# Other places in SBUF for the K, V and output-projection buffers of a cached attention step

## The chip, the cores and the metric

The kernel runs on one core of a Trainium2 chip. The core has a matrix engine (PE), a vector engine (DVE), a scalar engine (ACT), a general engine (POOL) and a queueing engine (SP), and 16 DMA engines that move data between device memory (HBM) and the on-chip memory SBUF. SBUF has 128 partitions, and a tile occupies the same byte range in each of them. PE writes its results into PSUM, which is organised in banks.

The metric is the device time of one execution in microseconds (us). The kernel before took 670.23 us, the median of three runs from 670.22 to 670.27.

## The reference, cut to what matters

One decoding step of a transformer block is computed for four sequences (B = 4, one token each, width D = 512). A conditioning vector gives six modulation vectors. Attention has 32 heads of width 128 over a cache of 4096 keys and values per head and sequence; a gated MLP follows.

```
mod = (silu(c) @ w_mod)                       # six vectors sa, ca, ga, sb, cb, gb
h   = layernorm(x) * (1 + ca) + sa
q   = (h @ wq) as [B, 32, 1, 128]
p   = softmax(q . k_cache * 128**-0.5)        # k_cache, v_cache: [4, 32, 4096, 128], bf16
o   = p . v_cache
x   = x + ga * (o @ wo)
h   = layernorm(x) * (1 + cb) + sb
x   = x + gb * gmlp(h)                        # w_in [512, 1792], w_out [896, 512]
```

The two caches hold 134 MB each. They are read once, and each element is used once.

## The kernel before, in words

**Tiling.** Work on the caches is cut into 32 items (`NQ`), one for each group of four heads and each sequence. An item has 4 MB of K and 4 MB of V. Each is brought by one DMA: 128 partitions, 32 KB in each, contiguous in device memory. The last item's V comes in five pieces, and its K in two. There are two buffers for K (`kt`) and two for V (`vt`), used in turn; the first V buffer holds `w_mod` at the start and the second holds `wq`.

**Steps of an item.** `scores` multiplies a half of the K buffer in place by the broadcast query `qbc` on DVE, and PE adds up the products over the head's width with 16 matmuls against the identity, reading the K buffer in strides; this is done for both halves. `fold` reduces the result into 128 scores a partition. `softmax` is a chain of short DVE instructions with one exponential on ACT. `values` multiplies the probabilities with the V buffer in 32 matmuls; ACT copies the result out, and `diagonal`, `project` and `apply` carry it through the output projection, whose weights for a group of heads are in `wo_g` (for the last group in `wo_l`). The steps are staggered: in the pass of item i stand the scores of i, the values of i-1 and the projection of i-2.

**What sets the order.** A small recording layer (`Program`) keeps each engine's instructions in the order in which they are written and derives the waits from reads and writes of the same tile. No scheduler moves anything. All large loads are issued on SP's queue in the order K of item i+1, then `wo_g` in some items, then V of item i. A load waits on SP until the buffer that it overwrites has been read by PE. The waits follow from the tile names and the ranges inside a tile, not from where in SBUF a tile lies.

**Where tiles lie.** All tiles come from one pool with one buffer each, made in the order of the `sb.tile` calls; the pool puts them one behind the other in SBUF. A tile's place therefore follows from the sizes of the tiles made before it. In the kernel before, `kt` and `vt` are made first. The places in the built program, in bytes within a partition:

| tile | bytes | place before | modulo 512 |
|---|---|---|---|
| kt0, kt1 | 32768 each | 16512, 49280 | 128 |
| vt0, vt1 | 32768 each | 82048, 114816 | 128 |
| rows (c and x) | 1024 | 147584 | 128 |
| wo_g | 4096 | 161504 | 224 |
| wo_l0, wo_l1 | 2048 each | 165600, 167648 | 224 |
| qbc | 8192 | 170080 | 96 |
| win0, win1 | 10752, 3584 | 179872, 190624 | 160 |
| wout0, wout1 | 4096, 3072 | 194208, 198304 | 160 |

Line numbers in the profile are those of the kernel before. L136 is the helper that records every DVE, ACT and POOL instruction, L141 the one that records a load; L349 is a plain matmul, L355 a weight load by itself and L360 a matmul that follows it.

Of the kernel before, what the change touches and what calls it, by code (L numbers as in the profile page):

```python
# [7 lines left out]
BF16 = mybir.dt.bfloat16  # L8
# [218 lines left out]
def kernel(  # L227
# [17 lines left out]
    P = 128  # L245
    B, _, D = A_x.shape
    _, H, SK, DH = A_k_cache.shape
# [4 lines left out]
    NH = 4  # L252
    G = H // NH
    R = P // NH
    NT = SK // R
# [9 lines left out]
    sb = ctx.enter_context(tc.tile_pool(name="sb", bufs=1))  # L265
    pm = ctx.enter_context(tc.tile_pool(name="pm", bufs=1, space=bass.MemoryType.PSUM))

    def tile2(shape, dtype, name, n=2):
        return [sb.tile(shape, dtype, name=f"{name}{a}") for a in range(n)]

    kt = tile2([P, NT * DH], BF16, "kt")
    vt = tile2([P, NT * DH], BF16, "vt")
    rows = sb.tile([2 * B, D], BF16, name="rows")
    wb_t = sb.tile([1, 2], BF16, name="wb_t")
    ident = sb.tile([P, P], BF16, name="ident")
# [19 lines left out]
    rz_t = tile2([P, NH], F32, "rz")  # L295
    oT = sb.tile([P, NH, B], BF16, name="oT")
    oP = sb.tile([P, NH, B], BF16, name="oP")
    wo_g = sb.tile([P, NH, D], BF16, name="wo_g")
    wo_l = tile2([P, NH // 2, D], BF16, "wo_l")
    modT = sb.tile([P, 6, J, B], F32, name="modT")  # L300
    qbc = sb.tile([P, B, G, DH], BF16, name="qbc")
    x1b = sb.tile([P, 2, J, B], F32, name="x1b")
# [8 lines left out]
    win = [sb.tile([P, j1 - j0, F], BF16, name=f"win{a}") for a, (j0, j1) in enumerate(WJS)]  # L311
    JFS = [(0, 4), (4, JF)]
    wout = [sb.tile([P, j1 - j0, D], BF16, name=f"wout{a}") for a, (j0, j1) in enumerate(JFS)]


    banks = [pm.tile([P, 512], F32, name=f"bank{a}") for a in range(8)]
# [457 lines left out]
```

## Time and profile before

| what | value |
|---|---|
| median of three runs | 670.23 us |
| the profiled execution | 670.11 us |
| its span, first to last instruction | 668.3 us |
| PE busy | 420.4 us (63%) |
| DVE busy | 402.9 us (60%) |
| ACT busy | 41.3 us (6%) |
| main DMA queue | 12640 packets, 282.73 MB, 98.8% of 16 engines' span |
| mean rate | 423 GB/s |
| granted PE clock, mean | 0.772 |

The engines' busy times are sums over their instructions. The DMA share is the time that packets took, as a share of the time of 16 DMA engines. A packet is the part of a load that goes to one partition, and one DMA engine moves it. The chain of work that ended last is followed back from the last instruction, each step to what released it. A load's time to landing runs from its issue on the queue to its end, so the waiting behind other loads is in it.

### The profile page before, as it was taken

To read this page: it belongs to the slowest core of one execution; us is meant where nothing else is said; L and a number is where in the kernel's file an instruction comes from. 1 tells how busy PE (TensorE), PEld (TensorE's weight loads), DVE (VectorE), ACT (ScalarE), POOL (GpSimd) and SP (SyncE) were. 2 spreads that over 40 slices of the span, in tenths; PEclk is the share of its full clock that TensorE was granted. 3 is DMA by queue.
4 is the path that set the end of the run, shared out by engine and by line. 5 is a ranking of instruction groups with operands and counts; after the bars stand their busy time and mean duration, and the time that the engine had idled before them with its cause. 6 is when DMAs were issued, how large, how long until landed. Compare 5 with 4: busy or idle time off the path is not lost.

```text
span 668.3 us, 5909 instructions
## 1 busy us (share of the span) xinstructions
PE 420.4 (63%) x3024; PEld 94.2 (14%) x2065; DVE 402.9 (60%) x475; ACT 41.3 (6%) x115; POOL 3.2 (0%) x17
## 2 busy tenths in 40 slices
PE   2557776665576754576655667656557675557784
PEld 2201110011111101111001111101111110111124
DVE  2177766676456666555756654757655666655662
ACT  1200000000000000000000000000000000000002
POOL 1000000000000000000000000000000000000000
PEclk9988876767888767888766788766788876788885
DMA  9999999999999999999999999999999999999995
GB/s 377 430 426 430 436 430 430 429 437 426 431 431 437 430 426 431 435 430 426 435 435 430 430 431 435 430 428 431 437 428 430 431 437 426 431 431 437 422 410 198
DMA packets 12673, 282.90 MB, mean 423 GB/s; under 512 B 1388, under 2 KB 1908, under 8 KB 3956
## 3 DMA queue, kind: packets, MB, share of 16 engines
q1 hardware_dynamic: 12640, 282.73, 98.8%
q8 instruction: 7, 0.11, 0.1%
q14 instruction: 6, 0.05, 0.0%
q10 hardware_dynamic: 20, 0.01, 0.0%
HBM read 282.73 MB, written 0.00 MB: 423 GB/s over the span
## 4 chain that ended last, share of the span: by engine, by line
DMA 63%; PE 24%; DVE 12%; issue 0%; SPq 0%; ACT 0%; DVEq 0%
DMA kt<-in_A_k_cache_dram 58%; PE bank L360 23%; DVE kt L136 11%; DMA vt<-in_A_v_cache_dram 3%; DMA wout<-in_B_w_out_dram 1%; PE bank L349 0%; SPq L141 0%; DVE S L136 0%; DVE P L136 0%; ACT E L136 0%; DVE mx L136 0%; DVE nm L136 0%; DVE mT L136 0%; DVE hm L136 0%; DVE hb L136 0%
## 5 line engine op out<-in xcount | busy, mean ns | idle before, releaser
L360 PE MATMUL bank<-kt,ident 128*128 128x512 bf16 x1024 | 295.0, 459 | 180.9 <-DVE kt L136 180.9
L136 DVE TENSOR_TENSOR kt<-kt,qbc 128x8192 bf16<-128x8192 bf16 x64 | 282.7, 4420 | 86.6 <-DMA kt<-in_A_k_cache_dram 86.6
L136 DVE TENSOR_REDUCE S<-bank 128x64 f32<-128x512 f32 x64 | 44.3, 692 | 125.6 <-PE bank L360 125.6
L355 PEld LDWEIGHTS <-ident 128*128 128x128 bf16 x64 | 9.1, 142 | 359.4 <-issue 359.3
L349 PE MATMUL bank<-vt,P 128*32 128x512 bf16 x992 | 59.2, 380 | 0.5 <-DMA vt<-in_A_v_cache_dram 0.5
L349 PE MATMUL bank<-sel,osb 128*128 128x4 f32 x248 | 35.7, 267 | 29.4 <-ACT osb L136 25.0
L136 ACT ACTIVATE E<-S,nm 128x128 f32<-128x128 f32 x32 | 12.8, 401 | 568.3 <-DVE nm L136 568.3
L349 PEld LDWEIGHTS bank<-sel,osb 128*128 128x128 f32 x248 | 33.0, 207 | 41.9 <-ACT osb L136 36.9
L136 DVE TENSOR_TENSOR P<-E,mask 128x512 bf16<-128x512 f32 x32 | 22.2, 693 | 18.0 <-ACT E L136 18.0
L349 PEld LDWEIGHTS bank<-rs,ones_f 128*128 128x128 f32 x64 | 12.1, 190 | 104.8 <-issue 104.0
L349 PEld LDWEIGHTS bank<-vt,P 128*32 128x32 bf16 x992 | 23.6, 96 | 21.4 <-DMA vt<-in_A_v_cache_dram 0.6
L136 ACT COPY osb<-bank 128x512 f32<-128x512 f32 x31 | 17.5, 565 | 17.4 <-PE bank L349 17.3
L349 PE MATMUL bank<-vt,hbc 128*32 128x512 bf16 x128 | 8.9, 448 | 4.7 <-DMA vt<-in_A_wq_dram 4.7
L349 PE MATMUL bank<-oP,wo_g 128*128 128x4 bf16 x112 | 3.9, 165 | 10.2 <-DVE oP L136 10.2
L136 DVE RECIPROCAL rz<-bank 128x4 f32<-128x4 f32 x32 | 5.6, 176 | 7.3 <-PE bank L349 7.3
L136 DVE TENSOR_REDUCE mx<-S 128x1 f32<-128x128 f32 x32 | 9.2, 286 | 1.1
L349 PE MATMUL bank<-rs,ones_f 128*128 128x4 f32 x64 | 9.1, 212 | 0.0
L136 DVE STREAM_TRANSPOSE nm<-hb 128x32 f32<-128x32 f32 x32 | 6.8, 212 | 1.1
L136 DVE STREAM_TRANSPOSE mT<-mx 128x32 f32<-128x32 f32 x32 | 6.8, 212 | 1.1
L136 DVE TENSOR_SCALAR rs<-mask,rs 128x4 f32<-128x4 f32 x32 | 7.2, 224 | 0.0
L136 DVE TENSOR_REDUCE hm<-mT 128x1 f32<-128x32 f32 x32 | 6.0, 186 | 1.1
L136 DVE TENSOR_SCALAR hb<-hm 128x32 f32<-128x32 f32 x32 | 5.8, 181 | 1.1
(91 smaller groups left out, 75.5 us busy)
## 6 DMA issues: line engine op xcount, KB each, us to landing
kt<-in_A_k_cache_dram SPq DMA_DIRECT2D x31, 4096.0 KB, 25.8
vt<-in_A_v_cache_dram SPq DMA_DIRECT2D x31, 4096.0 KB, 33.1
vt<-in_A_wq_dram SPq DMA_DIRECT2D x1, 4096.0 KB, 20.5
kt<-in_A_k_cache_dram SPq DMA_DIRECT2D x2, 2048.0 KB, 24.7
wo_g<-in_A_wo_dram SPq DMA_DIRECT2D x7, 512.0 KB, 22.8
vt<-in_w_mod_dram SPq DMA_DIRECT2D x1, 3072.0 KB, 10.2
vt<-in_A_v_cache_dram SPq DMA_DIRECT2D x1, 2048.0 KB, 19.8
win<-in_B_w_in_dram SPq DMA_DIRECT2D x1, 1344.0 KB, 14.8
```

Source lines behind the costliest of these rows:

```text
L136: eng, lambda e: getattr(e, name)(*args, **kw), ins, outs, sem=sem, done=done, after=after,
L349: "PE", lambda e: e.matmul(out, lhsT=lhsT, rhs=rhs, start=start, stop=stop, **kw),
L355: prog.add("PE", lambda e: e.ldweights(lhsT), [lhsT], [], done=False)
L360: return e.add_instruction(mybir.InstMatmult(name=nc.get_next_instruction_name(), engine=mybir.EngineType.PE, ins=[e.lower_ap(rhs), e.lowe ...
```

## The change

Only the order in which tiles are made is changed, and with it their places. The small tiles, `qbc`, `win` and `wout` are made first; then a tile `fill` of 96 bytes that nothing reads or writes; then the two V buffers, the two K buffers, `wo_l` and `wo_g`.

```
-    kt = tile2([P, NT * DH], BF16, "kt")
-    vt = tile2([P, NT * DH], BF16, "vt")
     rows = sb.tile([2 * B, D], BF16, name="rows")
...
-    wo_g = sb.tile([P, NH, D], BF16, name="wo_g")
-    wo_l = tile2([P, NH // 2, D], BF16, "wo_l")
     modT = sb.tile([P, 6, J, B], F32, name="modT")
...
     wout = [sb.tile([P, j1 - j0, D], BF16, name=f"wout{a}") for a, (j0, j1) in enumerate(JFS)]
+    fill = sb.tile([P, 48], BF16, name="fill")
+    vt = tile2([P, NT * DH], BF16, "vt")
+    kt = tile2([P, NT * DH], BF16, "kt")
+    wo_l = tile2([P, NH // 2, D], BF16, "wo_l")
+    wo_g = sb.tile([P, NH, D], BF16, name="wo_g")
```

The places after it, in the built program:

| tile | place after | modulo 512 |
|---|---|---|
| vt0, vt1 | 62208, 94976 | 256 |
| kt0, kt1 | 127744, 160512 | 256 |
| wo_l0, wo_l1 | 193280, 195328 | 256 |
| wo_g | 197376 | 256 |
| rows | 16512 | 128 |
| qbc | 30816 | 96 |
| win0, win1 | 40608, 51360 | 160 |
| wout0, wout1 | 54944, 59040 | 160 |

## The prediction

> **What bounds the kernel now.** I read the chain of work that ended last first, then the DMA part of the page, then the windows of the steady stretch, and last what the DMA queue itself waits for. From the page:
>
> ```profile
> span 668.3 us, 5909 instructions
> ...
> DMA  9999999999999999999999999999999999999995
> ...
> DMA packets 12673, 282.90 MB, mean 423 GB/s; under 512 B 1388, under 2 KB 1908, under 8 KB 3956
> ## 3 DMA queue, kind: packets, MB, share of 16 engines
> q1 hardware_dynamic: 12640, 282.73, 98.8%
> ...
> DMA 63%; PE 24%; DVE 12%; issue 0%; SPq 0%; ACT 0%; DVEq 0%
> ...
> L360 PE MATMUL bank<-kt,ident 128*128 128x512 bf16 x1024 | 295.0, 459 | 180.9 <-DVE kt L136 180.9
> L136 DVE TENSOR_TENSOR kt<-kt,qbc 128x8192 bf16<-128x8192 bf16 x64 | 282.7, 4420 | 86.6 <-DMA kt<-in_A_k_cache_dram 86.6
> ...
> kt<-in_A_k_cache_dram SPq DMA_DIRECT2D x31, 4096.0 KB, 25.8
> vt<-in_A_v_cache_dram SPq DMA_DIRECT2D x31, 4096.0 KB, 33.1
> ```
>
> From the windows of the steady stretch (length, busy time of PE, PE loads, DVE, ACT and POOL, clock, DMA share, GB/s):
>
> ```profile
> 100.00:200.00 100.00, 63.44 (x402) 12.64 (x252) 62.27 (x67) 4.82 (x15) 0.00 (x0) 0.76 1.01 432
> 400.00:500.00 100.00, 61.77 (x402) 12.52 (x252) 60.95 (x67) 4.82 (x15) 0.00 (x0) 0.76 1.00 431
> ```
>
> From the DMA queue's own waits:
>
> ```profile
> SPq L141 <- PE bank L360: 511.5, 31, 27.6
> SPq L141 <- PE bank L349: 91.2, 31, 17.9
> ```
>
> The chain gives PE and DVE a third of the span, but that misleads. It steps from a landed K through multiply and matmuls to the release of the buffer, then into the next load of that buffer, whose 25.8 us are mostly queueing: a 4 MB load alone takes 9.7 us at 432 GB/s. So 16 us of other transfers stand before it, and the 16 DMA engines never stop: share 1.00 in every steady window, 98.8% over the span, while DVE and PE are busy 62 of 100 us. SP waiting for PE costs nothing as long as that queue is full. The kernel's time is the sum of packet times on one DMA engine, from 2 us to 663 us, with about 5 us of arithmetic behind. Any effect must come through the duration of a packet.
>
> **One packet, from the trace's records of single packets.** A 4 MB load is 128 packets of 32 KB, one per partition, eight on each engine. Shortest and mean durations on the main queue, in ns, with the start of the destination modulo 512 bytes (read off the built program):
>
> ```
> size     destination        start   shortest  mean
> 32768    K, V, wq           128     1213      1217.5
> 24576    w_mod              128      912       996
> 16384    K and V, last      128      611       616
>  4096    V, last            128      159       162
>  4096    wo_g               224      159       163
>  4096    wout0              160      159       163
>  2048    V, last            128       84        87
>  1024    wo_l               224       46        50
>  1024    c, x (eight)       128       44        83
>   256    code (other queue)          15        15
> ```
>
> From 16 KB to 32 KB the shortest grows by 602 ns, so the bytes move at 27.2 a ns, and 1213 - 1204 leaves a fixed 9 ns a packet. The rest of the mean, 4.5 ns, is a spread: the first 32 KB load (wq) is 1213 in all 128 packets, later ones mix 1213, 1218 and 1221. On each engine 504 packets have 32 KB; 8 x 1217.5 = 9.74 us, and successive steady loads start 9.71 us apart, so packets overlap by a few ns and a ns off a packet is a ns off its engine.
>
> **The change, part by part.**
> *Order of the work.* No instruction, wait, semaphore or issue is added, removed or moved on any engine or queue: the streams differ in places and in three extra source lines. The fill tile is never read or written. Cost 0, which needs no cover.
> *Small tiles and the other weights* (rows up to qbc and wout). They move down by 131072 bytes as a block and stand as before modulo 512: qbc at 96, win and wout at 160. The temporaries made later shift by 96 bytes; they are touched in microseconds at the two ends. Bounds: an instruction there is some 0.17 us by the rows of DVE, about twenty lie in the last 5 us, and 10% on all would be 0.3 us either way. I take 0.
> *Engines reading K and V.* The multiply in place has kt at 256 instead of 128 and qbc where it was. Its 64 instructions take 4412 to 4427 ns, whichever of two K buffers and two halves; matmuls from V have 379 ns at the median. No place but 128 appears, so the trace doesn't price another. It is hidden by the DMA queue: a pass is 19.4 us long (two loads) and holds 62% of that, 12.1 us, of DVE. The multiply would have to grow from 4.42 to over 8.0 us before DVE sets the pass. Taken at 0, with a loss bounded in the rivals.
> *DMA into K, V and wo.* This is the term. Packets whose start moves to 256 modulo 512, per engine: 504 of 32 KB, 8 of 24, 24 of 16, 8 of 8, 64 of 4 (8 V, 56 wo_g), 16 of 2, 32 of 1 KB: 656. win, two wout and the four little inputs keep their modulus. All shown starts (128, 160, 224) are off a multiple of 256; the trace holds no large packet on one. Upper gain: the whole fixed 9 ns, 656 x 9 = 5.9 us, and beyond it the spread, 504 x 4.5 = 2.3 us. Lower bound: the spread widens, all packets as the slower common value, 1221 instead of 1217.5: 504 x 3.5 = 1.8 us more; the two worst K/V loads average 1222, which on all would be 504 x 4.6 = 2.3 us more. Nearest rows for what the fixed part can shrink to: the 256-byte packets keep 15 - 9.4 = 5.6 ns, and the shortest 1 KB packets of c and x keep 44 - 37.6 = 6.4. The usual is 8.5 (159 - 150.5; 84 - 75.3 = 8.7; 46 - 37.6 = 8.4). I take the lowest, 5.6, so 2.9 ns a packet: 656 x 2.9 = 1.9 us saved. This is the softest step: the packets of c and x start at 128 themselves, so something other than the start can shorten the fixed part.
>
> Sum: the profiled execution took 670.11 us for its span of 668.3 us, 0.12 below the median of 670.23. 670.11 - 1.9 = 668.2; against the median, 668.3 us, 0.28% less.
>
> [...] The 4 KB packets have the same shortest time at 128, 160 and 224. [...]
>
> **The rivals.**
> *Nothing (places don't matter, or less than 1.3 us).* For it: the equal rows at three starts, and a stream already at 432 GB/s, 27.0 a ns an engine against 27.2. Against it: none of these starts is on 256. It gives 670.1 us, 669 to 671.5.
> *Slower: the landing side spreads.* Place: the 32 KB packets into K and V while DVE and PE read neighbouring K and V buffers, whose places all move. For it: packets are uniformly 1213 before the engines work and mixed later; the cause doesn't show. Against it: the second K load, moved from 29 to 39 us with DVE and PE already on the first, still has 115 of 128 at 1213. Price: 1.8 to 2.3 us, 672.0 to 672.5; it decides against no change once the mean of 32 KB packets is over 1220.1 (2.7 ns x 504 = 1.34 us). [...]
> *Much slower: the multiply loses its rate at the new place.* At twice 4.42 us, DVE would have 12.1 + 8.8 = 20.9 us a pass, 1.5 over the DMA's 19.4: about 30 x 1.5 = 45 us more, 715. Against it: its place moves by 128 bytes, by whole multiples of its element, and qbc stays.
> That the moves do not happen is excluded: the built program has K and V at 256 modulo 512.
>
> **How the numbers follow.** Forecast (fixed part shrinks): 0.43, its own range 666.3 to 668.9. Nothing: 0.35. Spread: 0.19, with its tail above 672.5. Multiply: 0.03. The bound for a difference is 0.2%, 1.3 us. So faster 0.43, same 0.35, slower 0.22. For 8 in 10 I go from 666.3 (4.0 us saved: half of the fixed 9 ns and half of the spread, 656 x 4.5 + 504 x 2.2) to 672.4, the upper end of the spread's price; the sides left out hold about 0.05 below and 0.10 above.
>
> **What would show it.** Right: the same instruction counts and chain; 32 KB packets with a shortest near 1210 and a mean near 1214.5; steady windows at 433 GB/s; multiply at 4.42 us and matmul from V at 379 ns; wo_g packets at 156; win and wout unchanged at 140 and 159. Nothing: shortest 1213 and mean 1217.5. Spread: shortest 1213, mean over 1220, windows at 430. Multiply: DVE over 90 of 100 us and DMA share below 1. I would be wrong outright if the steady DMA share fell while no packet lengthened, since then the queue ran dry and the cause is an engine.

## The result, and the profile after

The changed kernel took 666.87 us (median of five runs, 666.79 to 666.96) beside 670.22 us for the kernel before (670.09 to 670.27): a ratio of 0.995 with a 95% interval of 0.9937 to 0.9964. That is 3.35 us less, faster by 0.5%, where 1.9 us less had been forecast. The profiled execution took 666.79 us for a span of 665.0 us.

From the page of the kernel after, the lines that answer to those shown of before (the kernel is three lines longer ahead of them, so L363 is the L360 of before):

```profile
span 665.0 us, 5909 instructions
...
DMA  9999999999999999999999999999999999999995
...
DMA packets 12673, 282.90 MB, mean 425 GB/s; under 512 B 1388, under 2 KB 1908, under 8 KB 3956
## 3 DMA queue, kind: packets, MB, share of 16 engines
q1 hardware_dynamic: 12640, 282.73, 98.8%
...
DMA 62%; PE 24%; DVE 12%; issue 0%; SPq 0%; ACT 0%; DVEq 0%
...
L363 PE MATMUL bank<-kt,ident 128*128 128x512 bf16 x1024 | 293.0, 457 | 179.7 <-DVE kt L136 179.7
L136 DVE TENSOR_TENSOR kt<-kt,qbc 128x8192 bf16<-128x8192 bf16 x64 | 282.7, 4419 | 84.7 <-DMA kt<-in_A_k_cache_dram 84.6
```

From its windows, with the columns as before (length, busy times, clock, DMA share, GB/s):

```profile
50.00:250.00 200.00, 131.00 (x833) 23.90 (x505) 131.07 (x135) 9.64 (x30) 0.00 (x0) 0.77 1.00 433
250.00:450.00 200.00, 123.66 (x830) 24.77 (x530) 124.17 (x135) 9.63 (x30) 0.00 (x0) 0.76 1.00 434
```

The same two windows of the kernel before:

```profile
50.00:250.00 200.00, 132.01 (x827) 25.47 (x505) 130.42 (x135) 9.64 (x30) 0.00 (x0) 0.76 1.01 432
250.00:450.00 200.00, 124.17 (x812) 23.80 (x504) 123.20 (x132) 9.64 (x30) 0.00 (x0) 0.76 1.00 431
```

The structure has not moved: 5909 instructions, the same packets, the same multiply, a DMA share of 1.00. Only the rate is different, by half a percent, and it can just be seen in the last column. The single packets tell more. Shortest, mean (both in ns) and the share of packets above the shortest, for before and after:

```
size     destination   start      shortest      mean               above the shortest
                       before/after             before   after     before  after
32768    K, V, wq      128 / 256  1213 / 1213   1217.5   1213.6    77%     0.3%
 4096    wo_g          224 / 256   159 / 159     162.8    159.6    70%     0.2%
 1024    wo_l          224 / 256    46 / 46       49.7     46.0    63%     0%
 3584    win           160 / 160   140 / 140     146.1    141.3    66%     4%
 4096    wout0         160 / 160   159 / 159     162.6    159.2    69%     3%
```

The shortest packet is what it was in every size. What went is the spread above it, and it went for win and wout0 too, whose starts modulo 512 are unchanged. (The first tile of win comes as three packets of 3584 bytes a partition, the tiles of wo_l as two of 1024.)

The sum of packet times on one engine (all packets of the main queue, divided by 16) fell from 659.99 to 657.20 us, by 2.79 us: 1.96 in the 32 KB packets, 0.63 in the other moved sizes (24 KB 0.14, 16 KB 0.08, 8 KB 0.03, V's last and wo_g's 4 KB 0.20, 2 KB 0.05, 1 KB 0.12, rounded), and 0.20 in win and wout. The 0.14 us of the 24 KB packets (w_mod, the first load) can't be put down to the start: over all fourteen profiles these packets sum to 7.8 to 8.2 us on an engine, in no order of start, and the profile of the change happens to have the lowest sum. The last load packet ended 3.32 us earlier. The other 0.5 us is that the end belongs to the slowest of the 16 engines: before, 16 to 18 load packets are under way at once from 657 to 658.5 us, and from 661 to 662.8 us one (after, one from 658.25 to 659.5 us). The last load packet ended 2.8 us behind that sum before, and 2.3 us behind it after (start and gaps included).

### The profile page after: what moved, and what is told of

Read it like the earlier page. It is cut to its first block, busy times and chain, and to the rows that moved or that the text cites. A ratio compares the mean times of both kernels' runs of the same rounds, so it can differ in the third digit from the quotient of the medians.

```text
span 665.0 us, 5909 instructions
## 1 busy us (share of the span) xinstructions
PE 417.8 (63%) x3024; PEld 93.0 (14%) x2065; DVE 402.7 (61%) x475; ACT 41.2 (6%) x115; POOL 3.2 (0%) x17
## 4 chain that ended last, share of the span: by engine, by line
DMA 62%; PE 24%; DVE 12%; issue 0%; SPq 0%; ACT 0%; DVEq 0%
DMA kt<-in_A_k_cache_dram 58%; PE bank L363 24%; DVE kt L136 11%; DMA vt<-in_A_v_cache_dram 3%; DMA wout<-in_B_w_out_dram 1%; PE bank L352 0%; SPq L141 0%; DVE S L136 0%; DVE P L136 0%; ACT E L136 0%; DVE mx L136 0%; DVE nm L136 0%; DVE mT L136 0%; DVE hm L136 0%; DVE hb L136 0%
## 5 line engine op out<-in xcount | busy, mean ns | idle before, releaser
L363 PE MATMUL bank<-kt,ident 128*128 128x512 bf16 x1024 | 293.0, 457 | 179.7 <-DVE kt L136 179.7
L352 PE MATMUL bank<-sel,osb 128*128 128x4 f32 x248 | 34.2, 261 | 29.4 <-ACT osb L136 24.9
L352 PEld LDWEIGHTS bank<-sel,osb 128*128 128x128 f32 x248 | 31.5, 199 | 41.9 <-ACT osb L136 36.8
```

What stands on the lines that cost most here:

```text
L352: "PE", lambda e: e.matmul(out, lhsT=lhsT, rhs=rhs, start=start, stop=stop, **kw),
L363: return e.add_instruction(mybir.InstMatmult(name=nc.get_next_instruction_name(), engine=mybir.EngineType.PE, ins=[e.lower_ap(rhs), e.lowe ...
```

## The experiments

Three theories for the gain. A: what counts is whether K and V start on a multiple of 256 bytes. B: what counts is the region of SBUF, or the order of the buffers. C: it comes from wo_g and wo_l alone. Beside these stands the question where the spread arises: in the DMA engines, or where DVE and PE use SBUF at the same time.

**The changed order, off 256 again.** K, V and wo all start at 128 modulo 512.

```
-    fill = sb.tile([P, 48], BF16, name="fill")
+    fill = sb.tile([P, 240], BF16, name="fill")
```

> The changed order of tiles, but with a fill of 480 bytes, so that K, V and wo start at 128 modulo 512 again. Theory A (the start of K and V modulo 256 bytes makes the difference): as before, 670.2 us, the mean of 32 KB packets at 1217 ns, shortest 1213. Theory B (it is where in SBUF, or in which order, the buffers lie): as after the change, 666.9 us, packets at 1213.5. Theory C (only wo_g and wo_l matter): wo is off 256 here too, so 670.2 us as with A.

Measured: 670.09 us beside 670.13 before, ratio 0.9999 (0.9989 to 1.0008). 32 KB packets: shortest 1213 ns, mean 1217.46, 76% above the shortest. The whole gain is gone with the new order still in place. B falls.

**The order before, on 256.** K and V at 256, wo_g at 352, win and wout at 288 modulo 512.

```
+    fill = sb.tile([P, 64], BF16, name="fill")
     kt = tile2([P, NT * DH], BF16, "kt")
     vt = tile2([P, NT * DH], BF16, "vt")
```

> The order of before with 128 unused bytes in front, so that K and V start at 256 modulo 512 and everything else moves by 128 bytes (wo_g to 352, win and wout to 288 modulo 512, none on a multiple of 256). Theory A: 666.9 us, packets of 32 KB at 1213.5 ns. Theory B: 670.2 us, 1217. Theory C: 670.2 us, since wo is still off 256.

Measured: 667.14 us beside 670.13, ratio 0.9955 (0.9938 to 0.9971); mean of 32 KB packets 1213.58. 128 unused bytes in front of the K tiles do nearly all of what the change does. C falls: wo is off 256 here. A stands.

**V at 128, K at 256, and the mirror.** In the changed order, first

```
-    fill = sb.tile([P, 48], BF16, name="fill")
+    fill = sb.tile([P, 240], BF16, name="fill")
     vt = tile2([P, NT * DH], BF16, "vt")
+    fill2 = sb.tile([P, 64], BF16, name="fill2")
     kt = tile2([P, NT * DH], BF16, "kt")
```

> The changed order, V at 128 and K and wo at 256 modulo 512. Theory A in its simple form (each packet pays for its own start): half of the effect, 668.5 us, packets into V mixed at 1213 to 1221 with a mean of 1217 and packets into K at 1213. Theory A in another form (misaligned packets spoil the pace of all that follow): packets of both kinds are mixed, between 668.5 and 670.2 us. Theory C: 666.9 us.

Measured: 667.67 us, ratio 0.9962 (0.9948 to 0.9976); mean 1213.83 ns, and only 3% of the 32 KB packets above the shortest. Half of the large packets are misaligned, and hardly any of them is long. Neither form of A as written holds: such a packet does not pay for its own start, nor does it spoil all that follows. The mirror asks whether V is special:

```
     vt = tile2([P, NT * DH], BF16, "vt")
+    fill2 = sb.tile([P, 192], BF16, name="fill2")
     kt = tile2([P, NT * DH], BF16, "kt")
+    fill3 = sb.tile([P, 64], BF16, name="fill3")
     wo_l = tile2([P, NH // 2, D], BF16, "wo_l")
```

> The mirror of the run with V at 128 and K at 256: now V and wo at 256, K at 128. If it is the share and the alternation of such packets that counts, 667.7 us and a mean of 1213.8 ns, as in the mirror. If K's start is the one that matters, 670 us and 1217.

Measured: 667.79 us, ratio 0.9962 (0.9948 to 0.9977), mean 1213.73, 3% above the shortest. Neither tensor is special.

**The same loads without the attention's arithmetic,** at the places of before and then of after. The per-item calls are left out; loads, head and tail stay. The output is not the attention's.

```
-        scores(i, 0)
...
-        scores(i, 1)
...
-        values(i - 1)
...
-    values_last(NQ - 1)
```

> Places of before, but the attention's arithmetic is left out: no scores, softmax, values or projection, so no engine reads or writes K, V or wo between 31 us and the end; the same loads in the same order, each waiting only for the load two earlier into its buffer. If the spread of packets needs the engines' accesses to SBUF, all 32 KB packets are 1213 ns, and successive loads start 9.681 us apart. If it comes from the DMA engines and the start alone, they are mixed at 1213 to 1221 with a mean of 1217, 9.716 us apart.

> The control of the run without the attention's arithmetic (again no scores, softmax, values or projection), with the places after the change. The start alone should set the packets: 32 KB packets at 1213 ns, mean 1213.6, 9.681 us from load to load, and about 665 us where the same with 128 took 668.3. If the arithmetic had a share in the gain, the two would differ by less than 3 us.

Measured, one run each, at 128: 668.33 us, 80% of the 32 KB packets above the shortest, mean 1217.02, loads 9.713 us apart in the median. At 256: 665.32 us, 0.1% above the shortest, mean 1213.13, 9.681 us apart. From the page of the run at 128, busy times and a window of its steady stretch:

```profile
span 666.5 us, 893 instructions
...
PE 18.2 (3%) x325; PEld 11.2 (2%) x325; DVE 8.7 (1%) x52; ACT 10.6 (2%) x20; POOL 3.2 (0%) x17
```

```profile
200.00:300.00 100.00, 0.00 (x0) 0.00 (x0) 0.00 (x0) 0.00 (x0) 0.00 (x0) 0.50 1.00 430
```

The same lines of the run at 256:

```profile
span 663.5 us, 893 instructions
...
PE 17.9 (3%) x325; PEld 11.1 (2%) x325; DVE 8.7 (1%) x52; ACT 10.6 (2%) x20; POOL 3.2 (0%) x17
```

```profile
200.00:300.00 100.00, 0.00 (x0) 0.00 (x0) 0.00 (x0) 0.00 (x0) 0.00 (x0) 0.50 1.01 435
```

In these windows nothing but DMA runs, and at 128 the spread is there as before (80% above the shortest, 77% with the arithmetic). The move by 128 bytes is worth 3.0 us of span here (666.5 against 663.5), and 3.3 us in the whole kernel; with one run each, the 0.3 us between the two are not shown to be anything. So the engines' use of SBUF is not what makes the spread.

**Other starts: 0 and 320 modulo 512.** The fill of the changed order becomes 176 or 80 columns.

```
-    fill = sb.tile([P, 48], BF16, name="fill")
+    fill = sb.tile([P, 176], BF16, name="fill")      # or [P, 80]
```

> The changed order with K, V and wo at 0 modulo 512. If a start on any multiple of 256 is what counts: 666.9 us, 32 KB packets at a mean of 1213.6 ns, as with 256 modulo 512. If 256 modulo 512 is special: 670.2 us and 1217.

> The changed order with K, V and wo at 320 modulo 512, which is 64 past a multiple of 256. If the spread is the same wherever the start is off 256: 670.2 us and a mean of 1217 ns. If it grows with the bytes past the boundary: about half the effect, 668.5 us and 1215 ns. If a multiple of 64 is enough, 666.9 us; but 128 is one too, so that is not expected.

Measured at 0: 667.14 us beside 670.29, ratio 0.9953 (0.9937 to 0.997), mean 1213.51. At 320: 670.2 us, ratio 0.9998 (0.9989 to 1.0008), mean 1217.27; the packets are no longer mostly 1218 and 1221 but 1215 and 1222, 90% above the shortest, and the mean is what it was. So 256 modulo 512 is nothing special, a multiple of 64 is not enough, and 64 past the boundary (670.2 us) costs as much as 128 (670.09).

**Loads in pairs, and one aligned buffer of four.** Half the large packets misaligned left them at 1213. The theory formed on this: misaligned packets (those whose start is off a multiple of 256) lose their pace only when many follow one another on an engine, and aligned packets between them set it right. Three runs are on this. The trace does not name a packet's load, so the shares by load below are worked out from the order of the queue, 128 packets to a load. First, the first buffers of K and of V at 128, the second at 256, with unused columns between the four:

```
-    fill = sb.tile([P, 48], BF16, name="fill")
-    vt = tile2([P, NT * DH], BF16, "vt")
-    kt = tile2([P, NT * DH], BF16, "kt")
+    fill = sb.tile([P, 240], BF16, name="fill")
+    gap = 64, 192, 64
+    kv = []
+    for a, n in enumerate(("vt0", "vt1", "kt0", "kt1")):
+        kv.append(sb.tile([P, NT * DH], BF16, name=n))
+        if a < 3:
+            sb.tile([P, gap[a]], BF16, name=f"gap{a}")
+    vt, kt = kv[:2], kv[2:]
```

> The first buffer of K and of V at 128, the second of each at 256, so that loads come as two misaligned and two aligned in turn (16 packets an engine of each kind), half of all packets misaligned as in the runs with V or K at 128. If misaligned packets drift apart as they follow one another and aligned ones set it right: more than with single alternation, 667.9 to 668.6 us, mean 1214 to 1215.5 ns, the mixed packets mostly in the second misaligned load of a pair. If only the share counts: 667.7 us, 1213.8 ns.

Measured: 667.74 us, ratio 0.9961 (0.9946 to 0.9975), mean 1213.73. In time it equals single alternation, so the time does not support the higher forecast. The packets do: with the first eight loads left out, the share above the shortest is 1% in the first misaligned load of a pair (V), 10% in the second (K), 4% in the aligned load that follows and 0% in the next. Then three misaligned loads to one aligned:

```
-    fill = sb.tile([P, 48], BF16, name="fill")
+    fill = sb.tile([P, 240], BF16, name="fill")
     vt = tile2([P, NT * DH], BF16, "vt")
-    kt = tile2([P, NT * DH], BF16, "kt")
+    kt = [sb.tile([P, NT * DH], BF16, name="kt0")]
+    gap = sb.tile([P, 64], BF16, name="gap")
+    kt.append(sb.tile([P, NT * DH], BF16, name="kt1"))
```

> Only the second K buffer at 256, both V and the first K at 128: three misaligned loads in a row (24 packets an engine), then an aligned one. Drift and repair: 668 to 668.8 us, mean 1214 to 1215.3 ns, mixed packets rarest in the first misaligned load after the aligned one, commonest in the third. If every misaligned packet paid on its own: three quarters of the effect, 669.4 us.

Measured: 668.53 us, ratio 0.9977 (0.9967 to 0.9986), mean 1215.28. The share above the shortest is 8% in the first misaligned load, about 60% in the second, 78% in the third, and 9% in the aligned one, where the unbroken stream before has 82%. The growth within a run of misaligned loads, and the repair by one aligned load, are shown here. These shares mix two cases, for wo_g is aligned in this run too and stands ahead of about every second of these V loads. Where it does, the three misaligned loads have 1%, 40% and 79%; where it does not, 15%, 80% and 77%. So a small aligned load (eight packets of 4 KB an engine) also repairs. The first loads of the kernel before, all at 128, show the same growth more slowly: wq has 0% above the shortest, the two K loads next 5% and 10%, V 24%, the next K 59%. In the run at 128 without the attention's arithmetic these five have 0%, 5%, 8%, 23% and 62%, so the growth does not come from the arithmetic either. Where wo_g does not stand ahead, the second misaligned load has 80% here, and 18% in the run with pairs, where two aligned loads lie between: one aligned load does not undo all of it.

Last, alternation without any aligned large load:

```
-    fill = sb.tile([P, 48], BF16, name="fill")
+    fill = sb.tile([P, 80], BF16, name="fill")
     vt = tile2([P, NT * DH], BF16, "vt")
+    fill2 = sb.tile([P, 160], BF16, name="fill2")
     kt = tile2([P, NT * DH], BF16, "kt")
+    fill3 = sb.tile([P, 64], BF16, name="fill3")
     wo_l = tile2([P, NH // 2, D], BF16, "wo_l")
```

> No large load aligned, but two different starts in alternation: V at 320 and K at 128 modulo 512, wo at 256. If the repair in the half-aligned runs comes from aligned packets: 670.1 us, mean 1217 ns. If it comes from a change of start from load to load: 667.7 us, 1213.8 ns.

Measured: 669.54 us, ratio 0.9991 (0.9981 to 1.0), mean 1216.87, 71% above the shortest. A change of start alone does not repair. The 0.6 us that are left of the gain go with wo_g, which is aligned here: the V loads that stand right behind it have 18% to 29% above the shortest, 23% in the mean, the other V loads of the same buffer 82% to 95% in the steady stretch, and the K loads that come next after the former are back at 74% to 82%. A run with wo_g off 256 here, which would test this by itself, was not made.

**Everything on 256,** the unused 96 bytes ahead of win instead of behind wout:

```
+    fill = sb.tile([P, 48], BF16, name="fill")
     win = [sb.tile([P, j1 - j0, F], BF16, name=f"win{a}") for a, (j0, j1) in enumerate(WJS)]
...
-    fill = sb.tile([P, 48], BF16, name="fill")
```

> The unused 96 bytes moved ahead of win, so that win and wout start at 256 modulo 512 too; K, V and wo stay at 256. Theory A with drift: packets of win and wout are nearly all at their shortest already (140 and 159 ns after the change), so within 0.2 us of 666.9. If each of their packets paid for its own start, 0.2 us less, hardly to be measured; packets of 3.5 and 3 KB at 140 and 121 ns throughout.

Measured: 666.83 us beside 670.13, ratio 0.995 (0.9933 to 0.9966). Packets of win have a mean of 141.1 ns instead of 141.3, those of wout's second tile 121.0 instead of 121.4. It is no faster than the change by anything that can be measured, and no version beat the changed kernel clearly.

## Why the prediction was right in its sign, and where its working was wrong

**What bounds the kernel: right.** The steady DMA share stays at 1.00, the multiply at 4.42 us, the matmul from V at 379 ns in the median, and DVE at 62 to 66% of the windows. The engines' terms, taken at zero, were zero as far as the runs can tell. Leaving out the attention's arithmetic takes only 1.8 and 1.5 us off the two spans (668.3 to 666.5, 665.0 to 663.5), which shows how well it is hidden.

**The fixed part: the step that failed.** "I take the lowest, 5.6, so 2.9 ns a packet: 656 x 2.9 = 1.9 us saved." The fixed part did not move: 1213, 159, 84 and 46 ns before and after, and in all twelve runs the usual shortest 32 KB packet is 1213. This term is 0. The 5.6 ns had been read off 16 packets of 256 bytes, which the prediction's table calls code on another queue; the trace has them on the main queue from 666.3 us on, and they are the store of the output, which goes the other way. The prediction itself also noted that the packets of c and x start at 128 and have a smaller fixed part (the shortest of them took 44 ns, the shortest of wo_l's 46); that note should have sunk the term.

**The spread: right term, left out of the sum.** It stood there as "beyond it the spread, 504 x 4.5 = 2.3 us". It delivered 3.9 ns on 504 packets, 1.96 us. With 0.63 us in the other moved sizes (0.14 of it w_mod's, which is not shown to come from the start), 0.20 in win and wout and some 0.5 from the slowest engine, that is the 3.3 us by which the profiled execution became shorter. The forecast of 1.9 us was close to 1.96 only because two different terms happened to have like sizes. That the time lies in the stated range is owed to its low end, which had put half of the spread beside half of the fixed part; by its own terms that end is 666.2 us, not 666.3.

**win and wout: wrong.** They were taken to stay, since their starts modulo 512 stay. (With qbc, they moved down by 139264 bytes, not 131072; the modulus is as stated.) Their shortest packet stayed, but their mean fell (146.1 to 141.3, 162.6 to 159.2). They come right behind wo_l, which is aligned after the change. Where wo_l is aligned and V is not (the run with V at 320), still only 4% of win's packets are above the shortest; where V is aligned and wo_l is not (the order before, on 256), 42% are. For win, then, the load just ahead counts most. For wout0, which comes behind win, that does not hold: with wo_l aligned in both, 52% of its packets are above the shortest in the run with V at 320, and 3% after the change. Why V's start shows there and not in win is open.

**The rivals.** "Nothing" rested on equal shortest packets at 128, 160 and 224. The rows were right, but the shortest packet could not show it: in these runs the start shows only in the spread, and there the table had no large load on a multiple of 256 to compare with. "The landing side spreads" had the spread in its sights and the cause wrong. Its condition was DVE and PE at work beside the packets; without them 80% of packets are still long. Its counter-row, a second K load with 115 of 128 at 1213 while DVE was at work, pointed the right way: the spread grows with the misaligned loads that have gone before, and at that time these were few, with DVE (10% above the shortest) or without it (8%).

**The price of a start, and the engines' side.** As a price of each packet by its own destination's start the effect does not show: the shortest 32 KB packet stays 1213 ns at 0, 256, 128 and 320 modulo 512, and with half of the large packets misaligned 97% are at the shortest. That a multiple of 256 is the place to aim at was the author's assumption, since the trace of before holds no large packet on one. The runs agree that the boundary of 256 counts: 0 and 256 are good (667.14 and 666.87 us), 128 and 320 are not (670.09 and 670.2 us). That DVE and PE would slow the packets does not show either: without the arithmetic the mean at 128 is 1217.0 ns, with it 1217.5, and the gain is 3.0 us of span against 3.3.

**What stays open.** The runs show that more of the misaligned packets are long the more of them follow one another, and that aligned ones undo it. They don't show what accumulates, nor where: in the DMA engines, on the way or at SBUF's side, nor why the mean ends near 1217 for both 64 and 128 past the boundary. In the half-aligned kernels 0.8 to 0.9 us against the change remain, of which the 32 KB packets' means explain only 0.1 (504 x 0.2 to 0.3 ns) and the packet sums 0.3 to 0.5, or 0.1 to 0.3 without w_mod; much of the rest lies in how far the slowest engine lags (the last load packet ends 2.8 to 3.0 us behind the sum there, 2.3 after the change), which was not taken apart.

## What to carry to other kernels

In a kernel that is bound by large loads into SBUF, look at the places of the destination tiles: here a start on a multiple of 256 bytes was worth 0.5%, for 96 or 128 unused bytes. Read a bound stream by the distribution of its packets, not by its mean rate alone: shortest and spread are two different costs, and an edit can touch one and leave the other (here the shortest stayed at 1213 ns and the mean went from 1217.5 to 1213.6). Some aligned loads among misaligned ones did much of the work (one large load in two gave three quarters of the gain, one in four half of it, wo_g and wo_l being aligned in both), so a test that moves only some tiles would have misjudged the effect.

## What the runs showed of the hardware that was not expected

- The start of a destination modulo 256 does not change the shortest packet (1213 ns for 32 KB at 0, 256, 128 and 320 modulo 512). It changes how many are longer: 0.1% to 0.3% on a multiple of 256, 76% to 90% off it, when all large loads are alike.
- How many are long depends on the loads that went before. With three misaligned loads and one aligned in turn, the share of long packets goes 8%, about 60%, 78%, and back to 9% in the aligned load. An aligned load of only 4 KB a packet (wo_g) takes the V load behind it from 89% to 23% where no large load is aligned.
- Packets of win, 3.5 KB each and themselves misaligned, came out short behind aligned ones: 4% of them above the shortest instead of 66%, with 512 aligned packets of 1 KB ahead of them.
- Single packets of 1.3 to 1.9 us occur in all runs of the whole kernel, 8 to 13 among the 8064 of 32 KB, and 2 in each of the two without arithmetic. What causes them was not tried.
